# Dense work of the last batch spread over seven blocks instead of nine, a gather and a list moved forward, one engine's count read last

## The chip, the cores and the metric

The kernel runs on one core of one Trainium2 chip. The metric is the device time of one execution in microseconds (us); smaller is better. Seven things work side by side on the core: TensorE (PE: matmuls and transposes, with its weight loads shown apart as PEld), VectorE (DVE), ScalarE (ACT), GpSimd (POOL), SyncE (SP) and the DMA engines that SP and POOL give work to. Each engine runs its own list of instructions in order, and they wait for each other through semaphores.

## The reference

Attention in which each query sees only its six best chunks of 32 keys, and behind it a mixture of experts: every token goes through one dense two-layer network and through the one expert that its gate picks.

```python
# attention: 4 batches, 8 heads, 768 tokens, head size 64
ub = np.sum(np.maximum(q * k_min, q * k_max), axis=-1)      # per query and chunk of 32 keys
top_chunks = np.argsort(ub, axis=-1)[..., -top_k:]          # top_k = 6
...
x = attn_out.transpose(0, 2, 1, 3).reshape(B * S, H * D)    # 3072 tokens x 512
# mixture of experts: 8 experts, 512 -> 512 -> 512
y_dense = np.maximum(x @ w1_dense, 0.0) @ w2_dense
expert_idx = np.argmax(x @ w_gate, axis=1)
for e in range(E):
    mask = expert_idx == e
    h = np.maximum(x[mask] @ w1[e], 0.0)
    y_moe[mask] = gate_w[mask, None] * (h @ w2[e])
return y_dense + y_moe
```

## The kernel before, in words

**Attention and routing, 0 to about 162 us.** Sixteen pairs of heads are worked off. What belongs to the experts is fitted in between as small functions ("pieces"). For each batch, `batch_fills` makes them: six transposes of x (`xtr`), the gate (`gate`), the rank of each token within its expert (`ranks`), six scatters that put the batch's rows into a table in DRAM sorted by expert (`place`, line 390), and 28 dense pieces (`l1`, line 410, and `l2`, line 426: halves of a first or second layer). An `l1` piece is two matmuls of 128x384, an `l2` piece two of 128x512. The second of two `l2` pieces ends a dense result: ACT copies it to `ys` (line 431), and SP writes it to the output in two DMAs (line 435). The last batch's pieces can't be hidden behind attention, since attention is over by then: they run among the blocks.

**Blocks, about 162 to 236 us.** The table is read back in blocks of 128 rows of one expert. There are at most 31 (`NBLK`); blocks 28 to 30 (`RARE` = 3) lie behind `tc.If(total > N2 - RARE)` (line 964) and don't run with these inputs, so that blocks 0 to 27 do. The first 11 (`N1`) were full before the last batch and are known early; the list of the other 20 (`N2`, "the second list") is known only after the last batch's ranks. Blocks are numbered from 0 here, as in the code: "scatter 8" of the change's short name is that of block 7, and its "blocks 2 to 8" are 1 to 7. For block i the main loop (line 937) emits, in this order:

- `fetch` (line 500): SP reads 128 table rows into a buffer `xg`, some blocks ahead. There are 13 such buffers; the 14th fetch waits until the scatter of block 0 has landed, and so on. The last block, 27, has a buffer `xl` of its own and is fetched first of the second list. Line 938 says how far ahead: before block 8 (`READY`) up to the 11 blocks of the first list, from then on three more a block.
- `own(i+1)` (line 515): DVE copies the next block's expert weights, 128x2048, to `w`.
- `e1(i)` (line 871): 16 matmuls to `hp`; ACT makes `ehT` of it (line 874).
- `tx(i+1)` (line 862): four transposes of the next block's rows; DVE copies them to `exT` (line 864).
- `extra[i]`: the pieces set down for this block (lines 929 to 932).
- `e2(i-1)` (line 892): four matmuls 128x512 to `yp`, with the weights' place taken from registers of PE; ACT scales them with the gate to `yo` (line 899, five buffers); POOL issues an indirect DMA that adds the 128 rows to the output (line 901, "scatter").
- `load_offs` (line 482): once, in block 8, PE and DVE read the second list's experts from SBUF to registers.

`dense_rows(27)` (line 879) is emitted in block 12, behind the scatter of block 11. POOL gathers the rows that block 27's tokens have in the output so far into `dr` (line 884), and the last scatter can then write (`yo` = yp * gate + `dr`, on DVE, line 897) instead of add. The gather may run only when all dense results have landed in the output. Scatters are declared free of each other and of the gather, and those of blocks 0 to 10 also of the last batch's dense writes; the gather is not. The count of blocks that are left, `total`, is read by every engine in block 9 (line 960) and used by line 964.

A Tile framework puts the instructions in order on each engine; it follows the order of emission but may pull something forward where an engine would wait. POOL's order around the gather is fixed by `tc.issue_after(latest["pool"].ins)`.

The lines that carry the change:

```python
for n, f in enumerate(d):                              # d: the 28 dense pieces
    extra.setdefault(1 + n * (N1 - 2) // len(d), []).append(f)
...
while got < min(i + AHEAD + 2 + (i >= READY), NOFT, N1 + 3 * max(i - READY + 1, 0)):
```

With N1 = 11 the first gives block 1 four pieces and blocks 2 to 9 three each.

Of the kernel before, what the change touches and what calls it, by code (L numbers as in the profile page):

```python
# [7 lines left out]

# [9 lines left out]
def kernel(  # L18
# [12 lines left out]
    nc = tc.nc  # L31
# [25 lines left out]
    N1 = (N * (B - 1) // B - E * 127 + 127) // 128  # L57
    N2 = NBLK - N1
# [107 lines left out]
    nblk = const.tile([1, 1], mybir.dt.int32)  # L166
# [82 lines left out]
    def apart(dma, group, reason):  # L249

        if group in groups:
            tc.declare_no_dep(dma.ins, group=group, reason=reason)
        groups.add(group)
        tc.add_to_no_dep_group(group, dma.ins)
# [227 lines left out]
    def load_offs():  # L482

        for have, engine in ((offs, mybir.EngineType.PE), (offs1, mybir.EngineType.DVE)):
            have.extend(unpack((eo, eparts[engine]), EF, 3, NK * 512, engine, (E - 1) * NK * 512,
                               "the expert of a block is at most the last"))
# [7 lines left out]
    def fetch(i):  # L494
        if i == NBLK - RARE - 1:
            xg = eg.tile([128, XW], U16, name="xl", bufs=1)
        else:
            xg = eg.tile([128, XW], U16, name="xg")
        es[i]["x"] = xg
        ld = nc.sync.dma_start(out=xg, in_=table[bass.ds(rows[i], 128)])  # L500
        if i < N1:
            tc.add_to_no_dep_group("full", ld.ins)
# [5 lines left out]
    def own(i):  # L508
        if i < 1:
            w = eg.tile([128, NK, 512], HF, name="w1a", bufs=1)  # L510
        else:
            w = later[0].tile([128, NK, 512], HF, name="w1", bufs=2)
        es[i]["w1"] = w
        with tc.issue_after(latest["xT"].ins) if "xT" in latest else nullcontext():
            nc.vector.tensor_copy(w.rearrange("p j f -> p (j f)"), w1f[:, bass.ds(offs1[i], NK * 512)])  # L515

    FIRST = 6
    with (
# [131 lines left out]
        h = None  # L650
        for d16, src in ((k16, s0["k"]), (q16, s0["q"])):
            o = d16.rearrange("p t g d -> p g t d")
            nc.gpsimd.tensor_copy(o[:, :, 0:3], src[:, :, 0:3])
            with after(h) if h else ExitStack():
                h = nc.scalar.copy(o[:, :, 3:6], src[:, :, 3:6])
            if src is s0["k"]:
                with after(h):
                    h = nc.scalar.copy(kT[0][0][64:128], exf)
# [27 lines left out]
        def place_k(p, g, pk):  # L686
            return nc.scalar.copy(kT[p][g][64 * g : 64 * g + 64].rearrange("d (T p j) -> d T p j", p=128, j=NJ),
                                  pk[64 * g : 64 * g + 64].rearrange("d (T j p) -> d T p j", p=128, j=NJ))
# [9 lines left out]
        with after(h):  # L698
            h = nc.scalar.activation(qp, pq, AF.Relu)
# [4 lines left out]
        for g in range(2):  # L704
            with after(h):
                h = place_k(0, g, pk)
        with after(dv):
            prep_ub(0)
        with after(h):
            h = nc.scalar.copy(kT[0][1][0:64], exf)  # L710
# [26 lines left out]
        with after(scored[-1][1]):  # L737
            h = nc.scalar.activation(qp, pq, AF.Relu)
# [106 lines left out]
    with (  # L845
# [8 lines left out]
        a, d, ranks, places, _ = batch_fills(B - 1)  # L854
# [3 lines left out]
        def tx(i):  # L858
            s = es[i]
            tp = p1.tile([128, NK, 128], HF, name="tp", tag="tr")  # L860
            for ko in range(NK):
                nc.tensor.transpose(tp[:, ko], s["x"][:, ko * 128 : (ko + 1) * 128].bitcast(HF), ident)  # L862
            s["xT"] = xT = et.tile([128, NK, 128], HF, name="exT")
            latest["xT"] = nc.vector.tensor_copy(xT, tp)  # L864

        def e1(i):
            s = es[i]
            hp = p2.tile([128, NK, 128], FP, name="hp", tag="h")
            for j in range(NK):
                for ko in range(NK):  # L870
                    nc.tensor.matmul(hp[:, j], s["w1"][:, ko, j * 128 : (j + 1) * 128], s["xT"][:, ko],  # L871
                                     start=(ko == 0), stop=(ko == NK - 1), skip_group_check=True)
            s["hT"] = h = et.tile([128, NK, 128], HF, name="ehT")
            nc.scalar.activation(h, hp, AF.Relu)  # L874

        def tokens(i):
            return bass.IndirectOffsetOnAxis(ap=es[i]["x"][:, Dm + 2 : Dm + 4].bitcast(mybir.dt.int32), axis=0)

        def dense_rows(i):

            es[i]["dense"] = dr = et.tile([128, Dm], FP, name="dr", bufs=1)
            nc.gpsimd.memset(dr, 0.0)
            with tc.issue_after(latest["pool"].ins):
                ga = nc.gpsimd.indirect_dma_start(out=dr, out_offset=None, in_=out, in_offset=tokens(i),
                                                  bounds_check=N - 1, oob_is_err=False)
            apart(ga, "add", "every token is in one block")

        def e2(i):
            s = es[i]
            yp = p3.tile([128, Dm], FP, name="yp", tag="y")  # L890
            for j in range(NK):
                nc.tensor.matmul(yp, s["hT"][:, j], w2f[:, bass.ds(offs[i] + j * 512, 512)],  # L892
                                 start=(j == 0), stop=(j == NK - 1))
            o = et.tile([128, Dm], FP, name="yo", bufs=5)
            gate, to = s["x"][:, Dm : Dm + 2].bitcast(FP), tokens(i)
            if "dense" in s:
                nc.vector.scalar_tensor_tensor(o, yp, gate, s["dense"], ALU.mult, ALU.add)
            else:
                nc.scalar.mul(o, yp, gate)  # L899
            with tc.issue_after(latest["put"].ins) if i == 0 else nullcontext():  # L900
                sc = nc.gpsimd.indirect_dma_start(out=out, out_offset=to, in_=o, in_offset=None, bounds_check=N - 1,  # L901
                                                  oob_is_err=False,
                                                  compute_op=ALU.bypass if "dense" in s else ALU.add)
            latest["pool"] = sc
            apart(sc, "add", "every token is in one block")
            if i < N1:
                tc.declare_no_dep(sc.ins, group="dense", reason="the first blocks hold no token of the last batch")
                tc.add_to_no_dep_group("add1", sc.ins)

        def empty():  # L910
# [7 lines left out]
            for e in range(E):  # L918
# [2 lines left out]
                apart(z, "rows", "these rows are no token's")  # L921
                tc.declare_no_dep(z.ins, group="full", reason="the first blocks end before these rows")

        AHEAD = 8
        READY = 8
        for i in range(1, 1):
            own(i)
        tx(0)
        extra = {0: a[:NT] + [a[NT], ranks], 1: list(places)}
        extra[2] = [empty]  # L930
        for n, f in enumerate(d):
            extra.setdefault(1 + n * (N1 - 2) // len(d), []).append(f)
        got = FIRST

        NOFT = NBLK - RARE
# [1 line left out]
        for i in range(NOFT):  # L937
            while got < min(i + AHEAD + 2 + (i >= READY), NOFT, N1 + 3 * max(i - READY + 1, 0)):
                if got < N1:
                    fetch(order[got])  # L940
                else:
                    with tc.issue_after(latest["ys"].ins):
                        fetch(order[got])
                got += 1
            if 1 <= i + 1 < NOFT:
                own(i + 1)
            e1(i)
            if i + 1 < NOFT:
                tx(i + 1)
            for f in extra.get(i, ()):  # L950
                f()
            if i > 0:
                e2(i - 1)
            if len(offs) < min(i + 4, NBLK):
                load_offs()
            if i == N1 + 1:
                dense_rows(NOFT - 1)
            if i == READY + 1:
                with tc.issue_after(latest["rows"].ins):
                    total = nc.values_load_multi_w_load_instructions(  # L960
                        nblk, min_val=0, max_val=N2, bass_reorder=False,
                        skip_runtime_bounds_check_because="the blocks that are left are at most N2")[1][0]
        e2(NOFT - 1)
        with tc.If(total > N2 - RARE):
            for i in range(NOFT, NBLK):
                fetch(i)
                latest.pop("xT", None)
                own(i)
                tx(i)
                e1(i)  # L970
                e2(i)
# [30 lines left out]
```

## Time and profile before

| | |
|---|---|
| median of 3 executions | 244.67 us (244.41 to 244.91) |
| the profiled execution | 245.93 us, of which the span from first to last instruction is 244.2 us |
| PE busy | 209.5 us (86% of the span) |
| DVE busy | 175.8 us (72%) |
| ACT busy | 174.3 us (71%) |
| POOL busy | 161.5 us (66%) |
| granted TensorE clock, mean | 0.987 |

In the profile a row of the timeline gives start and length in us, the engine, the line of the kernel, the operation, what it writes and reads, how many instructions were merged, and in brackets how long the engine was idle before and what ended that. A row of the chain (the work that ended last, followed back) gives start, length and what. A row of a view by stretches gives for each engine busy time and instructions, the granted clock, the busy share of the 16 DMA engines and GB/s. "q" behind an engine's name marks its sequencer: it waits, reads registers or issues DMAs. All times are from the span's start.

### The profile page before, as it was taken

The numbers are of one execution on the slowest core, as the hardware profiler recorded it, in microseconds if no ns is written. First come the engines' busy times: TensorE is split into PE (matmuls) and PEld (weight loads), VectorE is DVE, ScalarE is ACT, GpSimd is POOL, SyncE is SP. The second block draws the span as 40 slices with busy tenths as digits, with TensorE's granted clock in tenths as the row PEclk, the third lists the DMA queues.
The fourth block names the chain that finished last, engine by engine and source line by source line (L and its number), as shares of the span: only waits on it lengthen the run. The fifth ranks groups of instructions, "written<-read, shape, count | busy, mean of one in ns | idle before, by whom it ended". The sixth has DMA issues, their size and how long they took to land. (4 is left out here: it accounts for less than half of the span.)

```text
span 244.2 us, 7889 instructions
## 1 busy us (share of the span) xinstructions
PE 209.5 (86%) x2771; PEld 149.2 (61%) x2771; DVE 175.8 (72%) x561; ACT 174.3 (71%) x325; POOL 161.5 (66%) x213
## 2 busy tenths in 40 slices
PE   0688788798997989997999997989999989999950
PEld 0466465575765667764667764767566657777720
DVE  3889999999989789796888997677732235555510
ACT  4579798888787899596899886844556556666630
POOL 6458784887288767359878828520688647888881
PEclk9999999999999999999999999999999999999995
DMA  6999999899689899999999999356489999988785
GB/s 176 255 248 281 215 253 262 235 203 219 169 138 347 156 298 223 256 198 225 317 169 261 194 178 226 111 154 182 142 268 223 215 279 235 185 152 117 90 117 109
DMA packets 68279, 50.55 MB, mean 207 GB/s; under 512 B 29712, under 2 KB 61328, under 8 KB 68240
## 3 DMA queue, kind: packets, MB, share of 16 engines
q0 software_dynamic: 15232, 19.32, 48.3%
q1 hardware_dynamic: 53008, 30.72, 45.9%
q8 instruction: 23, 0.38, 0.6%
q14 instruction: 16, 0.13, 0.2%
HBM read 41.93 MB, written 18.23 MB: 246 GB/s over the span
## 5 line engine op out<-in xcount | busy, mean ns | idle before, releaser
L610 ACT ACTIVATE ex<-sp 128x512 f16<-128x512 f32 (+1 forms) x176 | 91.7, 607 | 9.8 <-PE sp L606 8.1
L606 PE MATMUL sp<-rT,kT 128*128 128x128 f16 (+3 forms) x384 | 64.5, 261 | 3.9 <-ACT ex L610 1.1
L612 POOL TENSOR_SCALAR_AFFINE_SELECT ex<-ex 128x512 f16<-128x512 f16 x48 | 32.5, 688 | 37.1 <-ACT ex L610 35.1
L901 POOL DMA_INDIRECT out_dram<-yo,xg x27 | 43.9, 1626 | 12.9 <-issue 5.2
L625 PE MATMUL op<-v,ex 128*128 128x65 f16 x672 | 46.1, 194 | 6.7 <-POOL ex L612 3.2
L625 PEld LDWEIGHTS <-ex 128*128 128x128 f16 x672 | 36.4, 98 | 22.8 <-POOL ex L612 7.3
L390 POOL DMA_INDIRECT table<-xbig,slot x24 | 24.3, 1012 | 17.7 <-issue 17.7
L864 DVE COPY exT<-tp 128x512 f16<-128x512 f16 x28 | 11.8, 423 | 32.8 <-PE tp L862 28.6
L606 PEld LDWEIGHTS <-kT 128*128 128x128 f16 x384 | 28.5, 98 | 7.5 <-issue 4.7
L892 PE MATMUL yp<-we,ehT 128*128 x112 | 30.9, 378 | 0.4 <-ACT ys L431 0.2
L871 PEld LDWEIGHTS <-w 128*128 128x128 f16 x432 | 26.4, 98 | 7.8 <-issue 2.2
L871 PE MATMUL hp<-exT,w 128*128 128x128 f16 x432 | 29.2, 219 | 0.6 <-issue 0.6
L410 PE MATMUL hp<-xT,wd 128*128 128x384 f16 x128 | 28.9, 325 | 0.6 <-DVE xT L266 0.6
L899 ACT ACTIVATE yo<-yp,xg 128x512 f32<-128x512 f32 x27 | 18.6, 688 | 14.0 <-PE yp L892 13.5
L548 DVE TENSOR_REDUCE ks<-kp 128x24 f16<-128x768 f16 x28 | 25.4, 946 | 3.6 <-ACT kp L545 3.3
L426 PE MATMUL yp<-wd,hT 128*128 128x512 f16 x96 | 25.9, 378 | 0.3
L874 ACT ACTIVATE ehT<-hp 128x512 f16<-128x512 f32 x28 | 16.7, 598 | 12.2 <-PE hp L871 8.9
L415 ACT ACTIVATE hT<-hp 128x384 f16<-128x384 f32 x30 | 14.9, 498 | 11.0 <-PE hp L410 10.3
L515 DVE COPY w<-we 128x2048 f16 x27 | 18.8, 697 | 0.2 <-DVE exT L864 0.2
L636 DVE TENSOR_TENSOR xbig<-op,rs 128x384 f16<-128x384 f32 x32 | 17.6, 549 | 0.3
L431 ACT COPY ys<-yp 128x512 f32<-128x512 f32 x21 | 12.7, 606 | 6.0 <-PE yp L426 5.9
L892 PEld LDWEIGHTS <-ehT 128*128 128x128 f16 x112 | 10.2, 97 | 10.4 <-issue 3.7
(158 smaller groups left out, 370.6 us busy)
## 6 DMA issues: line engine op xcount, KB each, us to landing
we<-in_moe_w_dram POOLq DMA_DIRECT2D x16, 512.0 KB, 7.2
kf<-in_k_dram SPq DMA_DIRECT2D x32, 192.0 KB
qf<-in_q_dram SPq DMA_DIRECT2D x32, 192.0 KB
vf<-in_v_dram SPq DMA_DIRECT2D x32, 192.0 KB
out_dram<-ys SPq DMA_DIRECT2D x48, 128.0 KB
xg<-table SPq DMA_DIRECT2D x27, 136.0 KB
table<-zt SPq DMA_DIRECT2D x9, 136.0 KB
wd<-in_moe_w_dense_dram POOLq DMA_DIRECT2D x2, 512.0 KB
```

The source lines that it names most:

```text
L390: sc = nc.gpsimd.indirect_dma_start(out=table, out_offset=bass.IndirectOffsetOnAxis(ap=keep["slot"][:, t : t + 1], axis=0), in_=xbig[b % 2 ...
L410: nc.tensor.matmul(hp, wd[:, ko, j * 128 : (j + 1) * 128], xT[:, ko, g * G * 128 : (g + 1) * G * 128], start=(ko == 0), stop=(ko == NK - 1))
L426: nc.tensor.matmul(yp, hold["h"][:, j, i * 128 : (i + 1) * 128], wd[:, NK + j], start=(j == 0), stop=(j == NK - 1))
L515: nc.vector.tensor_copy(w.rearrange("p j f -> p (j f)"), w1f[:, bass.ds(offs1[i], NK * 512)])
L548: nc.vector.tensor_reduce(out=ks[:, i], in_=kp.rearrange("d (c w) -> d c w", w=32), op=op, axis=mybir.AxisListType.X)
L606: last = nc.tensor.matmul(sp[:, o : o + w], kT[p % NB][g][:, kt * 128 : (kt + 1) * 128], rT[p % NB][g][:, a * 128 : z * 128], start=(o == ...
L610: scored.append((last, nc.scalar.activation(ex[:, 0:o], sp[:, 0:o], AF.Exp, scale=-0.125)))
L612: latest["pool"] = nc.gpsimd.affine_select(out=ex, in_=ex, compare_op=ALU.is_ge, fill=0.0, base=0, pattern=[[0, 4], [1, 2], [2, 64]], chan ...
L625: nc.tensor.matmul(s["op", g][:, t * (D + 1) : (t + 1) * (D + 1)], ex[:, o : o + 128], v16[p % NB][:, g, kt, :], start=first, stop=(last_o ...
L871: nc.tensor.matmul(hp[:, j], s["w1"][:, ko, j * 128 : (j + 1) * 128], s["xT"][:, ko], start=(ko == 0), stop=(ko == NK - 1), skip_group_che ...
L892: nc.tensor.matmul(yp, s["hT"][:, j], w2f[:, bass.ds(offs[i] + j * 512, 512)], start=(j == 0), stop=(j == NK - 1))
L901: sc = nc.gpsimd.indirect_dma_start(out=out, out_offset=to, in_=o, in_offset=None, bounds_check=N - 1, oob_is_err=False, compute_op=ALU.by ...
```

## The change

Four edits:

- Dense pieces: `N1 - 4` instead of `N1 - 2`. Blocks 1 to 7 now have four pieces each, and blocks 8 and 9 have none.
- `dense_rows(27)`, with its gather, is emitted in block 8 (`N1 - 3`) instead of block 12, and so stands behind the scatter of block 7 on POOL, with those of blocks 8 to 11 behind it.
- `READY` is 6 instead of 8: the second list's fetches are emitted from block 6 on, and the count in block 7.
- The count is read by all engines but PE where it was; PE reads it behind the last block's `e2`. A helper joins the two register handles for line 964.

```diff
+        def count(engines):
+            return nc.values_load_multi_w_load_instructions(
+                nblk, engines=engines, min_val=0, max_val=N2, bass_reorder=False,
+                skip_runtime_bounds_check_because="the blocks that are left are at most N2")[1][0]
+
+        def both(a, z):
+            hs = [h for v in (a, z) for h in (v.val.handles if hasattr(v.val, "handles") else (v.val,))]
+            return RuntimeValue.of_register_unchecked(RegisterHandles(tuple(hs)), min_val=0, max_val=N2)
...
-        READY = 8
+        READY = 6
...
-            extra.setdefault(1 + n * (N1 - 2) // len(d), []).append(f)
+            extra.setdefault(1 + n * (N1 - 4) // len(d), []).append(f)
...
-            if i == N1 + 1:
+            if i == N1 - 3:
                 dense_rows(NOFT - 1)
             if i == READY + 1:
                 with tc.issue_after(latest["rows"].ins):
-                    total = nc.values_load_multi_w_load_instructions(
-                        nblk, min_val=0, max_val=N2, bass_reorder=False,
-                        skip_runtime_bounds_check_because="the blocks that are left are at most N2")[1][0]
+                    total = count([e for e in mybir.ALL_ENGINES if e != mybir.EngineType.PE])
         e2(NOFT - 1)
+        total = both(total, count([mybir.EngineType.PE]))
         with tc.If(total > N2 - RARE):
```

More of the change, by code (lines that the diff above doesn't have):

```diff
@@ L5 @@
 from concourse import bass_utils, mybir
+from concourse.bass_primitives_rust import RegisterHandles
+from concourse.expressions import RuntimeValue
 from concourse.masks import make_identity, make_upper_triangular
```

## The prediction

> **What bounds the kernel now.** First the page, then the chain of work that ended last, for the stretch of the blocks.
>
> ```profile
> PE 209.5 (86%) x2771; PEld 149.2 (61%) x2771; DVE 175.8 (72%) x561; ACT 174.3 (71%) x325; POOL 161.5 (66%) x213
> ```
>
> ```profile
> 195.35 1.29 PE yp L426 x6
> ...
> 197.78 0.65 issue
> ...
> 204.53 0.89 PE hp L871 x16
> 205.42 0.22 PE tp L862 x4
> 205.64 0.86 PE yp L892 x4
> ```
>
> A block without dense pieces is 0.89 + 0.22 + 0.86 = 1.97 us of matmuls, back to back; three `l2` pieces are 1.29, one 0.43. PE sets the pace, apart from the 0.65 in which it stood still. The view by stretches gives the blocks: 2 to 7, then 8, 9 and 10, and the DMA engines.
>
> ```profile
> 169.77:190.39 20.62, 20.60 (x190) 12.73 (x189) 9.56 (x36) 12.16 (x21) 15.33 (x12) 1.00 0.81 209
> 190.39:194.07 3.68, 3.44 (x32) 2.09 (x30) 1.02 (x2) 1.92 (x4) 2.54 (x2) 1.00 1.07 224
> 194.07:198.43 4.36, 3.71 (x32) 2.03 (x31) 1.02 (x2) 3.07 (x5) 1.55 (x1) 1.00 1.11 251
> 198.43:200.41 1.98, 1.98 (x25) 1.51 (x26) 0.67 (x2) 0.67 (x2) 1.55 (x1) 1.00 1.06 243
> 184.00:212.00 28.00, 27.11 (x288) 18.71 (x287) 10.88 (x22) 17.21 (x28) 19.72 (x13) 1.00 1.08 233
> ```
>
> From 184 to 212 the DMA engines are full (share 1.08). Behind block 10 a block takes 1.98. But the end is not PE's: it is POOL's, as its timeline shows (scatters of blocks 7, 12, 13, 19, 22, 23 and 27; the gather at 207.48).
>
> ```profile
> 195.23 1.55 POOL L901 DMA_INDIRECT out_dram<-yo,xg  x1 [2.00 <-ACT yo L899]
> ...
> 207.48 1.33 POOL L884 DMA_INDIRECT dr<-out_dram,xl  x1 [0.30 <-issue]
> 209.11 1.68 POOL L901 DMA_INDIRECT out_dram<-yo,xg  x1 [0.31 <-issue]
> 211.10 1.65 POOL L901 DMA_INDIRECT out_dram<-yo,xg  x1 [0.30 <-issue]
> ...
> 222.94 1.67 POOL L901 DMA_INDIRECT out_dram<-yo,xg  x1 [0.30 <-issue]
> ...
> 228.87 1.68 POOL L901 DMA_INDIRECT out_dram<-yo,xg  x1 [0.30 <-issue]
> 230.85 1.56 POOL L901 DMA_INDIRECT out_dram<-yo,xg  x1 [0.30 <-issue]
> ...
> 238.29 1.03 POOL L901 DMA_INDIRECT out_dram<-yo,xl  x1 [0.30 <-issue]
> ```
>
> ```profile
> 211.96 0.69 DVE L515 COPY w<-we 128x2048 f16 x1
> 220.41 0.69 ACT L899 ACTIVATE yo<-yp,xg 128x512 f32<-128x512 f32 x1 [0.43 <-PE yp L892]
> 223.84 0.68 DVE L515 COPY w<-we 128x2048 f16 x1
> 229.78 0.68 DVE L515 COPY w<-we 128x2048 f16 x1
> 234.04 0.69 ACT L899 ACTIVATE yo<-yp,xg 128x512 f32<-128x512 f32 x1 [0.21 <-PE yp L892]
> ```
>
> In block 7 POOL waits for ACT. From the gather on it never does: every scatter follows the one before after 0.30. The scatter of block 19 starts at 222.94, while its `yo` was done at 220.41 + 0.69 = 221.10, **1.84 later**. A free scatter takes 1.55, so that POOL's own pitch is 1.55 + 0.30 = 1.85, 0.12 a block faster than PE; it could catch up, but doesn't. The scatters that took 1.65 to 1.68 end just behind a weight copy on DVE: 211.10 + 1.65 = 212.75, the copy 212.65; 222.94 + 1.67 = 224.61, the copy 224.52. A scatter whose end would fall into a copy is held until 0.1 behind it, again one block later, and so on: POOL is **locked** 1.84 behind `yo`, until the copies stop (the last at 229.78) and it runs 1.86 a scatter to the end.
>
> The Trainium skill, "SBUF — State Buffer", section "SBUF: two separate sides", has a reason: VectorE and GpSimd share a port pair, which one of them locks for a whole instruction, and GpSimd can't write its descriptors meanwhile. Held for a whole copy, each scatter would take 0.68 longer and POOL 2.53 a block; the trace shows 0.12, so the sum goes by the trace.
>
> Which lags lock follows from the same rows. For block 19 a free end falls between 223.84 and 224.62 if the scatter starts 1.19 to 1.97 behind its `yo`, and the copies come every 1.98. So a lag below 1.19 melts to nothing; one of 1.19 to 3.17 ends at 1.84; one of 3.17 to 5.15 ends at **3.82**, a whole block later.
>
> **Part by part.** *The pieces.* Blocks 8 and 9 took 3.68 + 4.36 = 8.04; without pieces they are 2 x 1.98 = 3.96. The 4.08 between are six `l2` pieces, 2.58, the idle 0.65, and 0.85 of gaps. The pieces only move: blocks 2 to 7 become 20.62 + 2.58, and some 0.2 of the gaps comes along, so that block 8 starts at 169.77 + 23.4 = 193.2 instead of 190.39. Of the 0.85 I take 0.65 as saved, because blocks without pieces have no gap; the ends are 0 and 0.85.
>
> *The count.* Two register reads stand in PE's list here:
>
> ```profile
> L960 SPq TENSOR_LOAD <-nblk x1: 1180/1180/1180, 189.1 to 189.1; - x1
> L960 PEldq TENSOR_LOAD <-nblk x1: 961/961/961, 197.4 to 197.4; - x1
> ```
>
> ```profile
> L472 PEldq TENSOR_LOAD <-eo x1: 972/972/972, 191.3 to 191.3; - x1
> ```
>
> The count's 0.96 held PE for the 0.65 above. Behind the last `e2` it costs nothing: what hides it is the last scatter, which starts at 238.29 and lands only shortly before 244.2 (without that cover it would cost its 0.96). The list of experts, 0.97 in block 8, lay beside six matmuls of 0.215; with the pieces gone it is bare and costs between 0 (PE has enough queued) and the 0.65 of its like. I take 0.35. **PE's gain: 0.65 + 0.65 - 0.35 = 0.95**, between 0 and 1.5. Block 10 starts at 198.43 - 0.95 = 197.5.
>
> *The list sooner* changes nothing on SP's queue but the time: the same transfers stand in the same order, and block 11's rows, whose fetch is issued by 189 (the rows of SP below), are first used behind block 10's matmuls, from 198.43 on. Cost 0. The cover is those nine microseconds. The fetches of blocks 13 to 15, which stand before the last dense writes, wait for the landing of the scatters of blocks 0 to 2, five blocks back. The other engines' count stays where it is or comes earlier; SP's 1.18 stays ahead of the dense writes.
>
> *The gather.* It waits until the last dense write has landed, and scatters 8 to 27 are queued behind it on POOL. So I follow that write along SP's queue.
>
> ```profile
> 186.94 2.12 SPq L500 DMA_DIRECT2D xg<-table  x2
> 193.18 1.12 SPq L435 DMA_DIRECT2D out_dram<-ys  x2
> 194.71 2.22 SPq L500 DMA_DIRECT2D xg<-table  x3
> 197.04 2.44 SPq L435 DMA_DIRECT2D out_dram<-ys  x4
> ```
>
> Before, SP waited for ACT in front of these writes. Now the results are there sooner (the last at about 193.2, when block 7's `e2(6)` ends) and SP is late itself: it is done with block 12's fetch at 189.06, reads the count until 190.3, and then issues 1.12 + 2.22 + 2.44 with 0.5 between them, until 196.6. The last write is issued at 196.0. How long does it take to land? SP's writes show no landing, so I bound it by three neighbours: a table read in the chain, before the crowd; then, from the views of line 884 and of line 901, the time from issue to landing of the old gather and of the scatters, both in the crowd.
>
> ```profile
> 160.46 2.38 DMA xg<-table
> ```
>
> ```profile
> DMA to landing us min/median/max: 5.0/5.0/5.0
> ```
>
> ```profile
> DMA to landing us min/median/max: 4.7/6.3/8.0
> ```
>
> Between 2.4 and 6.3, the scatters' median, then. I take 5.0, the gather's: it too moves 128 rows of 2 KB once, in the same crowd. Landed at 201.0 (198.4 to 202.3). POOL itself is free sooner: `yo` of block 7 is done at about 196.1, its scatter runs from 196.4 to 198.0, and POOL then **stands still for some 2.7 us** in front of the gather. The gather ends at 201.0 + 1.33, and the scatter of block 8 starts 0.30 later, at 202.6. Its `e2` ends as block 10 begins, and 0.2 of latency and ACT's 0.69 bring its `yo` to 198.4. The lag is 4.2. At 0.12 a block it melts to 3.82 within four blocks and locks there: one block more than before. The old gather's 1.63 at 207.48 is gone, but it was part of the old lag and isn't counted again.
>
> *Sum.* PE -0.95; lag 3.82 instead of 1.84, +1.98; behind the last copy one scatter more runs at 1.86 instead of 1.98, -0.12. Together +0.91. The profiled execution took 245.93, its span 244.2 and 1.7 around it, so that it becomes 246.8; its 1.26 above the median of the runs is its own. On the median 244.67: **245.6**.
>
> **The rivals.**
> 1. *The write lands in time for the old lock* (faster, the other side). The point is a lag of 3.17: the scatter of block 8 at 201.6 or before, the write landed by 199.9, within 3.9 of its issue. Then the lag ends at 1.84 as before and PE's gain remains: 244.67 - 0.95 = 243.7. For it: SP's write is not an indirect one, and 2.38 was seen. Against it: share 1.08 around it, and scatters that take 6.3. The skill's "DMA: Bandwidth & Descriptors", section "Anatomy of one DMA — SWDGE (gpsimd) path", puts a DMA at a fixed 2.0 us plus its bytes; an estimate by that for 128 KB is 2.3, which would land it at 198.3 and give this rival, but the 5.0 of the gather, twice the size, speaks against it here.
> 2. *The lag melts*: the write lands within 2.5 and PE stands between `e2(7)` and `e2(8)` for the list of experts, so that the lag starts below 1.19. Then the last ACT `yo`, done at 234.73 before, is followed at once: the scatter of 26 at 235.1 instead of 236.4 (238.29 less one pitch), and the end 1.33 sooner: 242.4.
> 3. *PE gains nothing* (the gaps move along, the list costs 0.65) and the lag is 3.82: 244.67 + 1.86 = 246.5.
> 4. *It nets out*: PE's whole 1.5 with the late lock, 245.0, or rival 1 with little gain, 244.4: within the bound of 0.2%.
>
> **How the numbers follow.** A measurement of this kernel can tell 0.2%, about 0.49 us, from no change. The forecast, with a lag of 3.82 and 0.4 to 1.4 of PE's gain, has 0.50 and runs from 245.1 to 246.1; rival 1 has 0.23, rival 2 0.09, rival 3 0.08, rival 4 0.10. Slower by over 0.49, above 245.16: 0.45 of the forecast's 0.50 (the rest for gains near 1.4) and rival 3's 0.08, 0.53. Faster, below 244.18: 0.20 of rival 1 and rival 2's 0.09, 0.29. Within: 0.18. The range 243.4 to 246.5 leaves out rival 2, the lower end of rival 1 and half of rival 3, not quite 0.2.
>
> **What would show it.** Block 10's first matmul at about 197.5, with no idle 0.65 before it. POOL idle for 2 us or more between the scatter of block 7 and the gather, ended by a dense write. Behind that, scatters of 1.65 to 1.68 that start 3.8 behind their `yo` in blocks 14 to 22. If POOL waits for ACT again in the last blocks, rival 2 holds; if the lag is 1.8, rival 1. If PE itself is stopped because the five `yo` buffers run out behind a late POOL, the step on PE's gain is wrong.

## The result, and the profile after

| | before | after |
|---|---|---|
| median | 244.79 us (243.79 to 245.46, 6 runs) | 248.87 us (246.65 to 249.95, 6 runs) |
| ratio after / before | | 1.0149, 95% interval 1.0113 to 1.0185 |
| profiled execution, span | 245.93 us, 244.2 us | 249.56 us, 247.9 us |
| start of the last scatter | 238.29 us | 241.93 us |
| blocks 2 to 9 on PE | 28.66 us | 27.01 us |

The forecast, 245.6 us, had the side right and a quarter of the size: 1 us for some 4. The first view is POOL's timeline of the changed kernel (start, length, what, idle time before and what ended it): the scatter of block 7, the gather, the scatters of blocks 8, 9 and 27.

```profile
194.95 1.78 POOL L903 DMA_INDIRECT out_dram<-yo,xg  x1 [0.42 <-ACT yo L901]
203.46 1.23 POOL L886 DMA_INDIRECT dr<-out_dram,xl  x1 [6.73 <-DMA xg<-table]
204.99 1.68 POOL L903 DMA_INDIRECT out_dram<-yo,xg  x1 [0.30 <-issue]
206.97 1.64 POOL L903 DMA_INDIRECT out_dram<-yo,xg  x1 [0.30 <-issue]
...
241.93 1.03 POOL L903 DMA_INDIRECT out_dram<-yo,xl  x1 [0.30 <-issue]
```

The reader is to see one number, **6.73**: POOL stands that long in front of the gather, and from there on it never waits again; every scatter follows the one before after 0.30. So the end is the gather's start plus what is queued behind it. Before, the gather started at 207.48 with 16 scatters behind it; now it starts at 203.46, only 4.02 sooner, with 20. Four more scatters at about 1.95 are 7.8, and 7.8 less 4.02 is 3.8; the last scatter is 3.64 later.

Why so late? The next two answers are SP's timeline, and the view of the gather's line: the five waits in front of it, with the times at which the first and the last of them start.

```profile
184.92 1.35 SPq L502 DMA_DIRECT2D xl<-table  x1
186.54 1.87 SPq L502 DMA_DIRECT2D xg<-table  x2
189.76 1.65 SPq L437 DMA_DIRECT2D out_dram<-ys  x2
191.82 2.05 SPq L502 DMA_DIRECT2D xg<-table  x3
193.97 3.09 SPq L437 DMA_DIRECT2D out_dram<-ys  x4
197.84 5.17 SPq L502 DMA_DIRECT2D xg<-table  x5
```

```profile
L886 POOLq EVENT_SEMAPHORE x5: 17/43/43, 200.5 to 202.6; - x5
```

The last dense write is issued in the stretch that ends at 197.06, about 196.4, and the last of POOL's waits, 43 ns long, stands at 202.6. Taken as that write's landing, this is 6.2 from issue to landing; in the traces of e9, e11, e14 and e17 below, read the same way, it is 5.0 to 7.0. No row shows the landing itself. The gather starts another 0.86 behind that (0.8 to 0.9 in those four). (The row of the gather names the last DMA that landed ahead of it, a table read; by the kernel's order what it waits for are the dense writes.)

On PE the forecast's gain is there, and more of it: 22.54 + 4.47 = 27.01 for blocks 2 to 9. But PE is stopped later. First the view by stretches, then PE's timeline, then ACT's.

```profile
169.27:191.81 22.54, 22.52 (x203) 13.89 (x202) 9.48 (x36) 14.06 (x24) 15.81 (x12) 1.00 0.83 211
191.81:196.28 4.47, 4.11 (x49) 2.94 (x48) 1.68 (x4) 2.57 (x4) 2.89 (x2) 1.00 1.10 268
...
211.20:216.05 4.85, 4.82 (x28) 3.06 (x28) 1.02 (x2) 2.03 (x4) 4.24 (x3) 0.65 0.98 162
```

```profile
194.31 1.05 PE L873 MATMUL hp<-exT,w 128*128 128x128 f16 x16 [0.36 <-DVE w L517]
...
209.06 0.39 PE L864 MATMUL tp<-ident,xg 128*128 128x128 f16 x4
211.23 1.39 PE L894 MATMUL yp<-we,ehT 128*128 x4 [1.79 <-ACT ehT L876]
212.43 1.90 PE L873 MATMUL hp<-exT,w 128*128 128x128 f16 x16
```

```profile
196.48 0.69 ACT L901 ACTIVATE yo<-yp,xg 128x512 f32<-128x512 f32 x1 [0.43 <-DMA xg<-table]
...
209.71 0.69 ACT L901 ACTIVATE yo<-yp,xg 128x512 f32<-128x512 f32 x1 [3.76 <-DMA out_dram<-yo,xg]
```

In front of block 9 PE stands 0.36. The row names DVE's weight copy, which ends at 194.14; the bare read of the list, which the forecast put at 0.35, starts at 192.8 and takes 1.3 to 1.4, so that it ends there too, and the row can't tell the two apart. In e14, the same kernel once more, the stop is 0.79, and the copy has ended 0.60 before the matmul: there it is the read. Block 8's `yo` is done at 196.48 + 0.69 = 197.17 and its scatter starts at 204.99: a lag of 7.8, nearly four blocks. With five `yo` buffers that is too much: ACT waits 3.76 for a scatter to land, PE 1.79 for ACT, and PE then runs at a granted clock of 0.65 for 4.85 us (16 matmuls take 1.90 for 1.06). Whether this stop costs anything, or only shortens the lag of a POOL that is late anyway, the trace alone doesn't say.

For the numbers of the next section: in the first eight experiments ACT and PE stood for some microseconds around 174 to 184 in every kernel, and the kernel before took 253 to 254 us, so that those runs are read for POOL's waits and lags alone. A ratio leaves out the executions in a slower state that some fall into; a median doesn't.

### The profile page after: what moved, and what is told of

Same layout as the page of the kernel before. It is cut to its first block, busy times and chain, and to the rows that moved or that the text cites. A ratio compares the mean times of both kernels' runs of the same rounds, so it can differ in the third digit from the quotient of the medians.

```text
span 247.9 us, 7889 instructions
## 1 busy us (share of the span) xinstructions
PE 211.3 (85%) x2771; PEld 151.2 (61%) x2771; DVE 175.7 (71%) x561; ACT 174.1 (70%) x325; POOL 161.2 (65%) x213
## 5 line engine op out<-in xcount | busy, mean ns | idle before, releaser
L873 PEld LDWEIGHTS <-w 128*128 128x128 f16 x432 | 27.1, 100 | 7.3 <-DVE w L517 1.1
L873 PE MATMUL hp<-exT,w 128*128 128x128 f16 x432 | 29.8, 222 | 0.4 <-DVE w L517 0.4
```

## The experiments

**Theory A**: the standstill in front of the early gather sets the loss, since POOL works back to back from there to the end; PE's stop costs nothing more. **Rival B**: the stop and the slow clock behind it are half of the loss. **Rival C**: the four pieces a block and the list sooner cost the time, and the gather's place matters little. The ten runs without the standstill carry the argument. They come from more than one chip, so each is read against the kernel before beside it.

| run | kernel | median us | before beside it | ratio (95% interval) |
|---|---|---|---|---|
| e9 | changed, pieces in blocks 1 to 8 | 249.41 | 244.9 | 1.0155 (1.0112 to 1.0198) |
| e10 | as e9, gather behind scatter 11 | 245.99 | 244.9 | 1.0026 (0.9997 to 1.0054) |
| e11 | as e9, eight `yo` buffers | 249.82 | 244.9 | 1.0199 (1.0162 to 1.0237) |
| e12 | before | 245.31 | 244.9 | 0.9989 (0.9956 to 1.0021) |
| e13 | changed, gather behind scatter 11 | 243.43 | 244.76 | 0.9967 (0.993 to 1.0003) |
| e14 | changed | 248.82 | 244.76 | 1.0148 (1.0096 to 1.0201) |
| e15 | changed, no gather | 244.1 | 244.76 | 0.9941 (0.9904 to 0.9977) |
| e16 | before, PE's count last | 244.15 | 244.76 | 0.997 (0.9939 to 1.0001) |
| e17 | changed, gather behind scatter 9 | 245.36 | 244.6 | 1.0029 (0.9998 to 1.006) |
| e18 | before, pieces in blocks 1 to 7 | 248.77 | 244.6 | 1.0138 (1.0088 to 1.0188) |

**The gather back (e13), beside the changed kernel (e14).** One line of the changed kernel:

```diff
-            if i == N1 - 3:
+            if i == N1 + 1:
                 dense_rows(NOFT - 1)
```

> The changed kernel with only the gather behind the scatter of block 11, again, for a chip without the standstill of the first eight runs. Theory A: PE's gain of 1.65 to block 10 stays, no standstill of POOL behind block 8, lag 1.84 locked behind the gather: 1.4 to 2.0 us below the kernel before (about 243.2 where before takes 244.9). Rival C (pieces and list sooner give nothing or cost, as the 246.0 of the run with pieces in blocks 1 to 8 hints): 244.7 or more. If the chip shows the standstill of ACT and PE between 174 and 184, only the lag is read.

> The changed kernel itself on the same chip. Theory A: POOL stands over 4 us in front of the gather, 3 to 5 us slower than before and 4.5 to 6.5 slower than the run with the gather back. If PE is late by a standstill between 174 and 184, the gather waits under 1.5 us and it is within 1.5 us of the run with the gather back.

POOL of e13, from the gather on (and the last scatter), and of e14, from the scatter of block 7 on:

```profile
204.69 1.33 POOL L886 DMA_INDIRECT dr<-out_dram,xl  x1 [0.30 <-issue]
206.32 1.67 POOL L903 DMA_INDIRECT out_dram<-yo,xg  x1 [0.30 <-issue]
...
235.50 1.03 POOL L903 DMA_INDIRECT out_dram<-yo,xl  x1 [0.30 <-issue]
```

```profile
194.39 1.55 POOL L903 DMA_INDIRECT out_dram<-yo,xg  x1 [0.42 <-ACT yo L901]
203.25 1.31 POOL L886 DMA_INDIRECT dr<-out_dram,xl  x1 [7.30 <-DMA xg<-table]
...
241.64 1.03 POOL L903 DMA_INDIRECT out_dram<-yo,xl  x1 [0.30 <-issue]
```

Behind scatter 11 the gather waits for nothing, and it starts only 1.44 later than where it is emitted four blocks sooner. The place of one line is worth 248.82 - 243.43 = 5.4 us. Rival C falls. Theory A had expected e13 1.4 to 2.0 below before; it is 1.33 below by the medians and 0.3% by the ratio, whose interval just reaches 1, so the size falls a little short. In the traces PE's gain does reach the end: from the `yo` of block 0 to the last scatter it takes 65.9 in e13 and 67.6 in before (and in e12).

**In between (e17): the lock.** The same line with `N1 - 1`.

> The changed kernel with the gather behind the scatter of block 9, two blocks later than in the changed kernel and two sooner than before. The forecast's lock: the last dense write lands as late as ever, so that POOL stands some 3 us, the scatter of block 10 starts 3.9 behind its yo, and from there the lag stays at 3.8 until the copies stop, PE unstopped: one block more than with the gather behind block 11, 1.86 above its 243.43, 245.3. Rival E (POOL, faster than PE, makes the lag good): 243.2 to 244. Rival F (PE is stopped here too and the time goes up as in the changed kernel): 247 or more.

POOL of e17, from the scatter of block 9 on, and ACT's `yo` of block 10:

```profile
199.53 1.55 POOL L903 DMA_INDIRECT out_dram<-yo,xg  x1 [0.42 <-ACT yo L901]
203.48 1.31 POOL L886 DMA_INDIRECT dr<-out_dram,xl  x1 [2.40 <-DMA xg<-table]
205.09 1.69 POOL L903 DMA_INDIRECT out_dram<-yo,xg  x1 [0.30 <-issue]
...
238.10 1.03 POOL L903 DMA_INDIRECT out_dram<-yo,xl  x1 [0.30 <-issue]
```

```profile
200.55 0.69 ACT L901 ACTIVATE yo<-yp,xg 128x512 f32<-128x512 f32 x1 [0.43 <-PE yp L894]
```

The lag starts at 205.09 - 201.24 = 3.85 and, until the copies stop, is 3.8 again wherever ACT hasn't itself waited for a free `yo`: 245.36 against the 245.3 that the lock gives. (The two runs are from different chips; each taken against before beside it, e17 is 2.1 above e13, for the 1.86 that was expected.) A POOL that is faster by 0.12 a block makes nothing good here. The gather starts at the same time as in the changed kernel, 203.48, with 18 scatters behind it for 20. The pitch is nearly the same in these four traces:

| | gather | scatters behind it | first to last | pitch |
|---|---|---|---|---|
| before | 207.48 | 16 | 209.11 to 238.29 | 29.18 / 15 = 1.945 |
| e13 | 204.69 | 16 | 206.32 to 235.50 | 29.18 / 15 = 1.945 |
| e17 | 203.48 | 18 | 205.09 to 238.10 | 33.01 / 17 = 1.942 |
| after | 203.46 | 20 | 204.99 to 241.93 | 36.94 / 19 = 1.944 |

In the other runs without the standstill that have a gather it is 1.935 to 1.956, but for e11 with 1.896 (below).

**PE's stop (e9, e11).** The pieces spread over one block more, so that the last dense write comes late even on a chip where PE is late; then the gather back (e10), and eight `yo` buffers (e11).

```diff
-            extra.setdefault(1 + n * (N1 - 4) // len(d), []).append(f)
+            extra.setdefault(1 + n * (N1 - 3) // len(d), []).append(f)
...
-            o = et.tile([128, Dm], FP, name="yo", bufs=5)
+            o = et.tile([128, Dm], FP, name="yo", bufs=8)
```

> The changed kernel with the dense pieces in blocks 1 to 8 for 1 to 7, so that the last dense write comes some 2 to 3 us later against the scatter of block 7 and the early gather, as it did in the changed kernel's first profile. Theory A (what costs is POOL's standstill in front of the gather, which waits for the landing of the last dense write): POOL stands 2 to 5 us in front of the gather, the scatters behind it start 3.5 or more behind their yo, with no recovery but where PE is stopped, and the time is 2 to 4 us above the same kernel with the gather behind block 11. Rival E (the standstill melts, since POOL is faster than PE): within 0.7 us of it.

> As the run before, but the gather behind the scatter of block 11. Theory A: POOL doesn't stand over 1 us behind block 8's scatter, the gather follows at once, the lag behind it is 1.8 to 1.9 or, where PE's pitch is over 2.0, down to 1.3: within 1.5 us of the kernel before on this chip. Rival C (pieces and list sooner cost the time): as slow as the run before.

> The changed kernel with pieces in blocks 1 to 8, and eight yo buffers for five. Theory A (POOL works back to back from the late gather on): PE is not stopped by ACT behind the gather, the lag stays at its first value or locks at 3.8 or 5.8, and the time is within 0.7 us of the run with five buffers. Rival B (the stop and PE's slow clock behind it cost about half): 1 to 2 us faster than with five.

> The kernel before itself, for its trace on this chip. If the chip is again one on which it takes about 253: ACT and PE stand for 3 us or more between 174 and 184, as in the eight runs so far, blocks 2 to 9 take 33 to 35 us for the 28.7 of the first profile, and the lag behind the gather is 1.9 and goes down where PE's pitch is over 2.0. If it takes 245, no such standstill and the lag locked at 1.84.

POOL and PE's stop in e9, where the five buffers run out; POOL of e11 and PE's matmuls at the same place; then PE and the stretch around its stop in e14:

```profile
203.12 1.08 POOL L886 DMA_INDIRECT dr<-out_dram,xl  x1 [6.54 <-DMA xg<-table]
...
241.67 1.03 POOL L903 DMA_INDIRECT out_dram<-yo,xl  x1 [0.30 <-issue]
```

```profile
210.99 1.36 PE L894 MATMUL yp<-we,ehT 128*128 x4 [1.19 <-ACT ehT L876]
```

```profile
204.86 1.10 POOL L886 DMA_INDIRECT dr<-out_dram,xl  x1 [6.53 <-DMA xg<-table]
...
242.29 1.03 POOL L903 DMA_INDIRECT out_dram<-yo,xl  x1 [0.30 <-issue]
```

```profile
212.57 1.06 PE L873 MATMUL hp<-exT,w 128*128 128x128 f16 x16
...
213.68 1.03 PE L894 MATMUL yp<-we,ehT 128*128 x4
```

```profile
211.06 1.36 PE L894 MATMUL yp<-we,ehT 128*128 x4 [1.74 <-ACT ehT L876]
```

```profile
210.80:216.00 5.20, 4.68 (x48) 3.05 (x48) 1.34 (x3) 2.13 (x4) 4.59 (x3) 1.00 0.97 153
```

Behind the gather PE never stops with eight buffers, and the time is 249.82 against 249.41: nothing is won. But the two traces don't differ in this alone. In e11's the blocks begin 1.50 later (`yo` of block 0 is done at 170.74 for 169.24), and the gather starts 1.74 later. Counted from the gather to the last scatter, e9 takes 38.55 and e11 37.43, 1.12 less. Of that, 0.35 is won up to the start of block 10's scatter, at 208.63 in e9 and so before PE's stop, which begins at 209.80. By these traces the stop costs POOL 0.77 at the most, less than the 1 to 2 us that Rival B expected. (In e11 the lag starts at 6.66, between two of the places where it locks, and sinks to 5.8 before the copies stop; hence its pitch of 1.896.) The slow clock costs nothing: in e14 PE stood 1.74 and 0.81 but kept the clock at 1.00, and from the gather to the last scatter it takes 38.39, for 38.47 in the profile with the slow clock. So Rival B falls: PE had time to lose, because POOL was the later one. With the gather back the same kernel takes 245.99, 3.4 less, as expected, though POOL stood longer in e9 (6.54) than the 2 to 5 expected. (e12, the kernel before once more, is within its own spread, 245.31 beside 244.9, and its lag is 1.84 again.) That e10 shows no gain against before is at least in part not the gather's doing; its PE stands in front of block 9:

```profile
194.88 1.03 PE L894 MATMUL yp<-we,ehT 128*128 x4
197.10 1.05 PE L873 MATMUL hp<-exT,w 128*128 128x128 f16 x16 [1.19 <-issue]
```

Pieces until block 8 leave PE's read of the second list bare behind them (it is at 195.5 in this trace); in e13, where it comes at 192.3, only 0.28 are left of it. These 0.91 are less than half of the 2.15 by which e10 takes longer than e13 from the `yo` of block 0 to that of block 8; the rest is open.

**The parts by themselves (e16, e18).** The kernel before with only the change's `count` and `both`, and with only this line:

```diff
-            extra.setdefault(1 + n * (N1 - 2) // len(d), []).append(f)
+            extra.setdefault(1 + n * (N1 - 4) // len(d), []).append(f)
```

> The kernel before with only PE's count behind the last e2. By the term of the sum: the idle 0.65 before block 10's first matmul is gone and the end comes 0.65 sooner: 244.25 where before takes 244.9. Rival: the read of the experts' list, or ACT, ends the wait then and block 10 starts less than 0.3 sooner: 244.6 or more.

> The kernel before with only the dense pieces in blocks 1 to 7, again, for a chip without the standstill. If the list two blocks sooner costs and gives nothing, as the forecast has it: 0.3 to 1.0 below before. If it is what feeds PE behind the pieces: SP issues the last dense writes first and the rows of block 11 only behind them, PE stands 1.5 us or more for these rows behind block 10's matmuls and runs at a lower clock for some us: 1 to 4 us above before.

The count: blocks 2 to 9 take 168.28 to 196.15, 27.87 for 28.66, and the median is 0.61 lower, as forecast (its interval just reaches 1). The pieces alone lose 4.2 us. PE, SP and the stretch behind block 10's matmuls in e18:

```profile
197.80 1.05 PE L871 MATMUL hp<-exT,w 128*128 128x128 f16 x16
201.00 0.61 PE L862 MATMUL tp<-ident,xg 128*128 128x128 f16 x4 [2.15 <-DMA xg<-table]
201.40 1.92 PE L892 MATMUL yp<-we,ehT 128*128 x4
```

```profile
180.80 14.19 SPq L435 DMA_DIRECT2D out_dram<-ys  x12
195.41 0.36 SPq L500 DMA_DIRECT2D xl<-table  x1
196.05 23.10 SPq L500 DMA_DIRECT2D xg<-table  x16
```

```profile
200.00:205.65 5.65, 4.65 (x32) 3.08 (x33) 1.69 (x4) 1.28 (x2) 1.83 (x2) 0.70 1.07 283
```

SP issues all twelve dense writes first and the rows of block 11 only behind 196: PE stands 2.15 for them and then runs at 0.70. So the list two blocks sooner is not worth nothing, as I had it: it feeds PE behind the pieces. And it has a price. In the changed kernel SP is done with the dense writes at 197.06, in e18 at 194.99. Between the changed kernel's writes stand six fetches of the second list, whose rows (1.35, 1.87 and 2.05) are shown above; e18 has none there. The part that makes the pieces possible makes the gather's wait longer.

**Without a gather (e15).** The gather is left out, and the last scatter adds like the others.

```diff
-            if i == N1 - 3:
-                dense_rows(NOFT - 1)
```

> The changed kernel without any gather, the last scatter adding. Theory A with the lock: lag 0.3 to 0.6 from block 8 to 25, PE sets the end; 1.5 sooner for the lag, 0.5 later for the longer last scatter: about 1.0 below the run with the gather behind block 11, 242.0 to 242.6 where before takes 244.9. Rival D (a lag builds up without the gather too, or an adding last scatter lands a microsecond or more later): not below it.

POOL of e15, the scatters of blocks 13, 14 and 27:

```profile
208.35 1.55 POOL L903 DMA_INDIRECT out_dram<-yo,xg  x1 [0.43 <-ACT yo L901]
210.33 1.55 POOL L903 DMA_INDIRECT out_dram<-yo,xg  x1 [0.43 <-ACT yo L901]
...
235.83 1.55 POOL L903 DMA_INDIRECT out_dram<-yo,xl  x1 [0.30 <-issue]
```

From block 12 on POOL is never more than 0.64 behind ACT, and no scatter is held: each takes 1.55. So the lag of 1.84 comes from the gather's own 1.63, as the lock has it. The gain at the end is a miss: expected 0.9 below e13, measured 244.1 against 243.43 by the medians and lower by the ratios, which is no difference. The traces say why. From the `yo` of block 0 to the last scatter e15 takes 65.13 and e13 65.90, so that POOL does win 0.77. But e15's last scatter starts at 235.83 and the span ends at 243.3, 7.5 later; in e13 it is 235.50 and 241.3, 5.8. What is won on POOL is lost in the last landing.

**The eight runs with the standstill.** e1 and e6 are e13's kernel, e2 and e8 the changed kernel with eight buffers, e3 is e16's, e4 e18's, e5 the changed kernel, e7 e15's.

| run | median us | before beside it | ratio (95% interval) |
|---|---|---|---|
| e1, e6 | 254.16, 256.1 | 253.26, 253.73 | 1.0042 (1.0005 to 1.0079), 1.0138 (1.0066 to 1.0209) |
| e2, e8 | 254.1, 253.97 | 253.26, 253.73 | 1.0041 (1.0003 to 1.0079), 0.9983 (0.9945 to 1.0021) |
| e3 | 253.2 | 253.26 | 1.0008 (0.9971 to 1.0044) |
| e4 | 256.72 | 253.26 | 1.0134 (1.0086 to 1.0182) |
| e5 | 257.19 | 253.73 | 1.0171 (1.0113 to 1.0229) |
| e7 | 253.69 | 253.73 | 0.9998 (0.996 to 1.0036) |

> The changed kernel with one line as before: the gather behind the scatter of block 11 again (other three edits kept). Theory A (POOL's standstill of 6.73 in front of the early gather sets the end): POOL has no idle over 0.6 between the scatter of block 7 and the end, PE isn't stopped by yo buffers, scatters lock about 1.84 behind yo, PE's gain of 1.4 to 1.7 is all that remains: 242.6 to 243.5. Rival C (the pieces four to a block and the list sooner crowd the DMA engines and cost the time; the gather's place matters little): 246 or more.

> The changed kernel with eight yo buffers for five. Theory A (behind the late gather POOL works back to back and its start sets the end; PE's stop only shortens the lag): PE no longer stands still at 211 and keeps the granted clock at 1.00, but the lag of the scatters stays at 7 or more (about 7.8) and the time is within 0.6 of the changed kernel's: 247.8 to 249.5. Rival B (PE's stop and the slow clock behind it are half of the loss, 1.79): 246.5 to 247.3.

> The kernel before with only the count split: PE reads it behind the last e2. By the term of the sum: the idle 0.65 before block 10's first matmul is gone, all behind it comes 0.65 sooner with the same lag of 1.84: 244.1. Rival: the scatters behind the gather are not sooner, since POOL is behind already, or the phase of the weight copies changes the lag: within 0.2 of before, 244.6 to 245.0.

> The kernel before with only the dense pieces in blocks 1 to 7. By the term of the sum: gaps 0.65 saved, the list of experts bare for 0.35, so 0.3 sooner: 244.5. By the changed kernel's trace (gain to block 10 of 1.65, less the count's 0.65): 1.0 sooner, 243.8. Rival C (four pieces a block crowd ACT, SP and the DMA engines and delay the blocks): 245.5 or more.

> The changed kernel itself, beside the kernel before on the same chip as the next three, because in the first four experiments the chip took 253 us for the kernel before and every engine stood for some microseconds around 176 to 183, so that PE came to the early gather late and it hardly waited. Theory A: where before takes about 245 and PE isn't held up in blocks 2 to 4, POOL stands over 4 us in front of the gather and the changed kernel is 3 to 5 us slower than before; where before takes 250 or more and PE is late, the gather waits under 1 us and the two are within 1.5 us of each other.

> The changed kernel with only the gather behind the scatter of block 11 again, as in the first experiment. Theory A: where before takes about 245, POOL never stands over 1 us behind block 8, lag of the scatters 1.8 to 1.9 behind the gather, PE not stopped, and the time is before's less PE's gain, 1.0 to 2.0 us faster than before (242.8 to 243.8). Rival C (the pieces and the list sooner cost the time): within 1 us of the changed kernel.

> The changed kernel without any gather: the last scatter adds to the output like all others. Theory A with the lock (a lag of 1.9 comes from the gather's own 1.63 and stays because scatters are held by the weight copies): the scatters of blocks 12 to 25 start 0.3 to 0.6 behind their yo and POOL waits for ACT in every block; the end is 1.4 sooner for the lag and 0.5 later for the longer last scatter: about 0.9 faster than with the gather behind block 11. Rival D (POOL falls behind without the gather too): lag 1.2 or more, and not faster than with it.

> The changed kernel with eight yo buffers, as in the second experiment. Theory A (POOL works back to back from the late gather to the end and sets the end; PE's stop only shortens the lag): where before takes about 245, PE no longer stands near 211, its clock stays at 1.00, the lag stays at 7 or more, and the time is within 0.6 of the changed kernel's. Rival B (PE's stop and the slow clock behind it are half of the loss): 1.2 to 2 us faster than the changed kernel.

ACT's standstill in e5, and POOL from the scatter of block 7 on:

```profile
179.25 0.60 ACT L876 ACTIVATE ehT<-hp 128x512 f16<-128x512 f32 x1 [3.25 <-PE yp L428]
183.48 0.59 ACT L433 COPY ys<-yp 128x512 f32<-128x512 f32 x1 [3.63 <-remote]
```

```profile
205.13 1.55 POOL L903 DMA_INDIRECT out_dram<-yo,xg  x1 [0.42 <-ACT yo L901]
207.48 1.08 POOL L886 DMA_INDIRECT dr<-out_dram,xl  x1 [0.80 <-DMA xg<-table]
208.86 1.84 POOL L903 DMA_INDIRECT out_dram<-yo,xg  x1 [0.30 <-issue]
...
217.18 1.55 POOL L903 DMA_INDIRECT out_dram<-yo,xg  x1 [0.34 <-ACT yo L901]
```

Where PE is late, so is the scatter of block 7; the gather then waits 0.80, and POOL soon waits for ACT again. That is Theory A's condition seen from the other side, and e2 and e8, where the gather waited 0.47 in the first, could not show a lag of 7 for the same reason: both expectations missed. The lags came as expected in e6 (1.9 behind the gather) and e7 (0.3), and e4's PE waited 1.86 for table rows, as in e18. The medians fit no theory well: the changed kernel is 3.5 above before although its profile shows no late POOL, and the gather back (e1, e6) and the count alone (e3) aren't faster than before. The profiles are of the fastest of four executions in e5 (253.92) and in e6 (254.70), so they don't show what made the others slower. What made the standstill, and why e5 and e6 are slow there, is open.

## Why the prediction was wrong

- **What bounds the kernel**: right. POOL ends last, and its lag is locked a little behind the ends of DVE's weight copies: 1.84 in before and e13, 3.85 in e17, and none where the gather is missing. Between such places it isn't fixed: in e11 scatters of 1.64 let it sink by 0.04 a block. The Trainium skill, "SBUF — State Buffer", section "SBUF: two separate sides", has DVE, in a mode that takes both ports, and GpSimd exclude each other from one port pair for whole instructions; no row shows in which mode the weight copy runs, but the scatters of e15, none of which is held at 1.55, and those of 1.67 in e13 agree with a turn that costs only where the two meet.
- **PE's gain, 0.95**: the mechanism right, the size low. Blocks 2 to 9 gained 1.65 (28.66 to 27.01; in e14's trace it is about 1.1). The count is 0.79 of it in e16's trace (forecast 0.65), so that the pieces bring some 0.9 net where I had 0.30. The bare read of the list cost what I took, 0.36, but 0.79 in e14, above the 0.65 that I had as its most: that it fitted is luck.
- **The list sooner, cost 0**: wrong by itself. Without it the pieces lose 4.2 us (e18), and with it SP is done with the dense writes 2.07 later than without (197.06 for 194.99).
- **"POOL then stands still for some 2.7 us"** is the step that failed, in its size: 6.73 measured. The gather was to start at 201.0; it started at 203.46. Of the 2.46, 0.4 is the issue of the last write (196.4 for 196.0), 1.2 its landing (6.2 for 5.0, just within the bound of 6.3), and 0.86 the time from the last wait to the gather, which I had not counted at all. The rest of the 6.73 is POOL, free 1.3 sooner (194.95 + 1.78 = 196.73 for 198.0), since PE gained more, and the 0.3 by which 201.0 less 198.0 is more than 2.7. My own bound should have warned me: landed at 202.3, the scatter of block 8 starts at 203.9, a lag of 5.5, which by the rule of the lock ends not at 3.82 but another block later, at 5.80. The sum is then 247.6, above the whole range, and no rival had it. The estimate of 2.3 by the Trainium skill, "DMA: Bandwidth & Descriptors", section "Anatomy of one DMA — SWDGE (gpsimd) path", was farther off than the 5.0 or the 6.3; that section is on DMAs that GpSimd issues, and these writes are SP's.
- **The lag, 4.2, which melts to 3.82**: 7.8, of which 2.4 is the gather and 1.2 PE's earlier `yo`. It came down to 3.8 in the end, but because PE was stopped, not because POOL caught up.
- **The sum.** I took the change as PE's gain plus one block of lag. Its form wasn't at fault: with the measured gain of 1.65, and a lag that stays at the 7.8 of blocks 8 to 11 (three blocks of 1.98 above 1.84), it gives 244.67 - 1.65 + 5.94 - 3 x 0.12 = 248.6. But in the run the lag didn't stay there, since PE was stopped, so this sum is not what happened. Counted on POOL alone, which needs no lag, the forecast's own scatter of block 8 at 202.6, with 19 pitches of 1.944, puts the last scatter at 239.5; at the measured 204.99 it is 241.9. The 2.4 between them, on 245.6, makes 248.0 of the 248.87.
- **The `yo` buffers**, which I named as what would make it wrong, did run out and stopped PE, but by e9, e11 and e14 this cost at most some 0.8 us at the end.

Two versions of the changed kernel come out at or below before: with the gather behind scatter 11 (243.43, interval 0.993 to 1.0003) and without a gather (244.1, 0.9904 to 0.9977). The runs don't tell one from the other.

## What to carry to other kernels

An instruction that must wait for a far-off landing goes into an in-order queue where the landing is due, not ahead of it: whatever is queued behind it counts at the engine's full pitch, here 1.94 us for each scatter put behind the gather against 4.02 us by which it came sooner. If an engine never waits from some point to the end, forecast the end from that point by its own pitch, and leave the other engines' gains out of the sum. Before taking a part of a change as free, ask which other part would starve without it.

## What the runs showed of the hardware

A stop of PE of 1.79 us (after) or 2.15 us (e18) was followed by 4.85 us at a granted clock of 0.65 and 5.65 us at 0.70; stops of 1.74 and 0.81 us (e14) by a clock of 1.00 up to 240 us. The Trainium skill, "TensorE: Matmul & The Clock Gate", section "Part 1: The HAM clock gate (the "warmup" mystery)", has the clock fall after an idle window of about 3.4 us; here shorter stops did it, though not every time.

The last scatter ended the span 7.5 us after its start where it adds (e15; 7.9 in e7) and 5.8 us where it writes (e13; 5.5 to 6.4 in all the profiles where it does). Between e15 and e13, 0.52 of the 1.7 is its own time on POOL, 1.55 for 1.03, and the rest comes behind it.
